# The front of an attention and ELU-MLP kernel: two token tiles side by side, one batch ahead

## The chip, the cores and the metric

The kernel runs on one core of a Trainium2 chip. The metric is the device time of one execution in microseconds. The engines in the text are PE (matrix multiply), PEld (its weight loads), DVE (vector), ACT (activations), POOL (GpSimd, which also issues DMAs that cast) and SP (issues plain DMAs). Each engine works through its own queue in order and waits on semaphores.

## The reference

```python
# q, k, v: [8 batches, 8 heads, 576 tokens, 64], float32; w_in [512, 2048]; w_out [2048, 512]
scores = (q @ k^T) / 8                       # per batch and head
scores = where(|i - j| <= 32, scores, -1e9)  # sliding window, both sides
attn   = softmax(scores)
x      = (attn @ v), heads side by side      # [4608 tokens, 512]
h      = x @ w_in
g      = where(h > 0, h, exp(min(h, 0)) - 1) # ELU
out    = g @ w_out                           # [4608, 512] float32
```

## The kernel before

**Attention.** Queries go in blocks of 64 (`QB`), nine to a batch, and two blocks make a *pair*: 36 pairs of 128 tokens. A block of 64 queries sees 128 keys, so the window is one 128 x 64 product per head. For a pair, `scores` fills `psS` (16 small matmuls), ACT exponentiates into `pu`, DVE multiplies with a mask (`mask`, into `pm`), `pv` multiplies with V, which carries a column of ones for the sum, `normalize` divides (`rc`, `x_st`), `x_transpose` turns the result on PE and `x_evac` copies it into `xT`. Two pairs make the 256 tokens of one tile. The softmax takes no maximum away, and masked places are multiplied by zero.

V is held twice: `V_e` for even blocks, as loaded, and `V_o` for odd ones, shifted by 64 tokens. `rotate_v` makes `V_o` from `V_e` with two DMAs on SP's queue.

q and k are loaded as float32 by SP (`load_qk`, whole or in halves `HALF_A` and `HALF_B` of 288 tokens), cast to bf16 (`cast_qk`), transposed on PE in 96 x 96 pieces (`transpose_qk`, into a PSUM tile `ptx`) and copied into `qT` and `kT` on ACT or DVE. v and the weights are loaded and cast by DMAs that POOL issues (`load_v`, `load_w_in`, `load_w_out`; the weights in four chunks each). `gate` is a DMA of one element that SP issues when a certain weight chunk is in; what SP issues after it waits behind it.

**The MLP.** 18 tiles of 256 tokens, each in 8 steps; a step takes 256 of the 2048 middle columns. `mm1` makes 8 matmuls into `ps` (`psH`), ACT's exponential gives `e_sb`, DVE subtracts one (`m_sb`) and combines (`elu`, `g_sb`); `mm2` adds 4 matmuls of g and w_out to the tile's sum `psY`. After step 7 the sum is copied to `y_sb` by ACT and DVE and stored by SP.

**The order.** There is no scheduler: the order of the calls is the order on the engines. A table `tasks`, filled by `at(kk, slot, ...)`, hangs attention work into the steps of the MLP loop. In step kk the loop runs:

```python
    LAG = 2
    for kk in range(NSTEP + LAG):
        run(kk, "first")
        if 1 <= kk <= NSTEP:
            elu(kk - 1)
        run(kk, "dve")
        if kk < NSTEP:
            mm1(kk)
        run(kk, "mid")
        if kk >= LAG:
            mm2(kk - LAG)
        run(kk, "end")
```

`pair_at(i, kk)` spreads a pair over the steps kk to kk + 3. From pair 6 on, pair i starts at step 4(i - 2), so a pair runs every four steps.

Before the loop stand half A of batch 0, its transposes, and pairs 0 and 1, each finished before the next begins. Half B of batch 0 is cast and transposed at step 2, just ahead of that step's `elu` and `mm1`. Batch 1 is cast mostly on POOL, in steps 8 to 13.

Of the kernel before, what the change touches and what calls it, by code (L numbers as in the profile page):

```python
# [21 lines left out]
def kernel(  # L22
# [43 lines left out]
    xpool = ctx.enter_context(tc.tile_pool(name="xT", bufs=2))  # L66
    mpool = ctx.enter_context(tc.tile_pool(name="moe", bufs=3))
    opool = ctx.enter_context(tc.tile_pool(name="outs", bufs=2))
    psH_pool = ctx.enter_context(
        tc.tile_pool(name="psH", bufs=3, space=bass.MemoryType.PSUM))  # L70
    psY_pool = ctx.enter_context(
        tc.tile_pool(name="psY", bufs=1, space=bass.MemoryType.PSUM))
    psS_pool = ctx.enter_context(
        tc.tile_pool(name="psS", bufs=1, space=bass.MemoryType.PSUM))
    psT_pool = ctx.enter_context(
        tc.tile_pool(name="psT", bufs=1, space=bass.MemoryType.PSUM))
# [65 lines left out]
    for i in range(3):  # L142
        nc.vector.memset(V_e[i][0:32, 0], 0.0)
        nc.vector.memset(V_e[i][96:128, VS - 1], 0.0)
        nc.vector.memset(V_e[i][:, :, :, D:VD], 1.0)
        if i < 2:
            nc.vector.memset(kT[i][:, :, 0:WIN], 0.0)
            nc.vector.memset(kT[i][:, :, KW - WIN:KW], 0.0)

    load_qk(0, 0, HALF_A)  # L150
    load_qk(0, 1, HALF_A)
    for m in range(3):
        load_v(0, m)
    rotate_v(0, 0, 2)

    ident = cpool.tile([128, 128], BF16)
    make_identity(nc, ident)

# [21 lines left out]
    for ki, kk in enumerate(kinds):  # L180
        for z in range(2):
            nc.vector.tensor_copy(
                masks[:, ki, z, :], mk[:, "EFL".index(kk[z]), :])
# [8 lines left out]
    def cast_qk(b, which, hp, part, eng):  # L192
        z, nj = part
        n = H * nj * D
        s_ = qk_f[b, which][:, z * n + 2 * hp * nj * D:
                            z * n + (2 * hp + 2) * nj * D]
        s_ = _bap(s_, [s_.ap[0], [nj * D, 2], [D, nj], [1, D]])
        t = lpool.tile([SP_, SJ, 2, D], BF16, tag=f"b{which}", name="qkb",
                       bufs=4)
        qk_b[b, which, hp, z] = t  # L200
        d_ = _bap(t, [t.ap[0], [D, 2], [2 * D, nj], [1, D]])
        if eng is nc.scalar:
            nc.scalar.copy(d_, s_)
        else:
            eng.tensor_copy(d_, s_)  # L205

    def transpose_qk(b, which, hp, part, evac, pool=None):
        z, nj = part
        src = qk_b.pop((b, which, hp, z))
        if pool is None:  # L210
            pt = psT_pool.tile([128, SJ, SP_], BF16, tag="pt", name="ptx")
        else:
            pt = psH_pool.tile([128, 2 * 512], BF16, tag="psH", name="ptx")
            pt = _bap(pt, [pt.ap[0], [SP_, SJ], [1, SP_]])
        for j in range(nj):
            nc.tensor.transpose(  # L216
                pt[:, j, :], src[:, j, :, :], ident[0:SP_, 0:SP_])
        src_ps = _bap(pt, [pt.ap[0], [1, SP_], [SP_, nj]])
        n = SP_ * nj
        if which == 0:  # L220
            d = qT[b % 2][:, hp, z * n:(z + 1) * n]
        else:
            d = kT[b % 2][:, hp, WIN + z * n:WIN + (z + 1) * n]
        d = _bap(d, [d.ap[0], [nj, SP_], [1, nj]])
        if evac is nc.scalar:
            nc.scalar.copy(d, src_ps)  # L226
        else:
            nc.vector.tensor_copy(d, src_ps)
# [3 lines left out]
    def scores(i):  # L232
        psS = psS_pool.tile([128, 2, 512], FP32, tag="psS")
# [13 lines left out]
        st[i] = [psS, pu, None, None]  # L247

    def mask(i):
        psS, pu, _, _ = st[i]  # L250
# [6 lines left out]
    def pv(i):  # L257
        psS, pu, pm, _ = st[i]
# [23 lines left out]
    def x_transpose(i):  # L282
        psS, _, _, x_st = st[i]
        pt = psS_pool.tile([128, NDO, 128], BF16, tag="psS", name="psXT")
# [21 lines left out]
    for hp in range(HP):  # L306
        cast_qk(0, 0, hp, HALF_A, nc.vector)
        cast_qk(0, 1, hp, HALF_A, nc.scalar)
        transpose_qk(0, 0, hp, HALF_A, nc.scalar, psH_pool)
        transpose_qk(0, 1, hp, HALF_A, nc.vector, psH_pool)  # L310

    load_w_in(0)
    load_w_out(0)
    gate(w_in_at(0))
    for which in range(2):
        load_qk(0, which, HALF_B)
    for m in range(3, VS):
        load_v(0, m)
    rotate_v(0, 2, VS - 1)
    for c in range(1, 4):  # L320
        load_w_in(c)
        load_w_out(c)
    gate(w_in_at(3))
    for part in (HALF_A, HALF_B):
        for which in range(2):
            load_qk(1, which, part)
    for m in range(VS):
        load_v(1, m)
    rotate_v(1)
# [25 lines left out]
    for i in (0, 1):  # L355
        for fn in (scores, mask, pv, normalize, x_transpose, x_evac):
            fn(i)


    for hp in range(HP):  # L360
        at(2, "first", cast_qk, 0, 0, hp, HALF_B, nc.vector)
        at(2, "first", cast_qk, 0, 1, hp, HALF_B, nc.scalar)
        at(2, "first", transpose_qk, 0, 0, hp, HALF_B, nc.scalar)
        at(2, "first", transpose_qk, 0, 1, hp, HALF_B, nc.vector)
    at(2, "first", scores, 2)
    at(3, "dve", mask, 2)
    at(3, "mid", pv, 2)
    at(4, "dve", normalize, 2)
    at(4, "mid", x_transpose, 2)
    at(5, "dve", x_evac, 2)  # L370
    pair_at(3, 5)

    for hp in range(HP):
        at(8 + hp // 2, "mid", cast_qk, 1, 0, hp, HALF_A, nc.scalar)
        at(8 + hp // 2, "mid", cast_qk, 1, 1, hp, HALF_A, nc.gpsimd)
        at(9 + hp // 2, "mid", transpose_qk, 1, 0, hp, HALF_A, nc.scalar)
        at(9 + hp // 2, "mid", transpose_qk, 1, 1, hp, HALF_A, nc.scalar)
        at(12 + hp // 2, "mid", cast_qk, 1, 0, hp, HALF_B, nc.gpsimd)
        at(12 + hp // 2, "mid", cast_qk, 1, 1, hp, HALF_B, nc.gpsimd)
        at(14 + hp // 2, "mid", transpose_qk, 1, 0, hp, HALF_B, nc.scalar)  # L380
        at(14 + hp // 2, "mid", transpose_qk, 1, 1, hp, HALF_B, nc.scalar)
    pair_at(4, 10)
    pair_at(5, 13)
    for i in range(6, NPAIR):
        pair_at(i, HALF * (i - 2))
    for b in range(2, B):
        k0 = HALF * (first_pair(b) - 2)
        for hp in range(HP):
            for which in range(2):
                kk = k0 + HALF * (hp - 4) + 1 + 2 * which  # L390
                at(kk - 5, "mid", cast_qk, b, which, hp, WHOLE, nc.gpsimd)
                at(kk, "mid", transpose_qk, b, which, hp, WHOLE, nc.scalar)
        at(k0 - HALF, "mid", rotate_v, b)
        if b >= 3:
            kk = k0 - 8 * HALF
# [6 lines left out]
    psH, e_t, m_t, g_t, psY = {}, {}, {}, {}, {}  # L402

    def mm1(kk):
        t, s = kk // STEPS, kk % STEPS
        ps = psH_pool.tile([128, FG, TT], FP32, tag="psH")
# [23 lines left out]
    def mm2(kk):  # L430
        t, s = kk // STEPS, kk % STEPS
        if s == 0:
            psY[t] = [psY_pool.tile([128, D_MODEL], FP32, tag=f"psY{ts}",
                                    name=f"psY{ts}")
                      for ts in range(2)]
# [57 lines left out]
```

## Time and profile before

| | |
|---|---|
| device time, median of 3 | 379.85 us (378.91 to 381.76) |
| the profiled execution, its own time | 378.95 us |
| its span, first to last instruction | 377.2 us |
| PE busy | 328.4 us (87%) |
| DVE busy | 254.1 us (67%) |
| ACT busy | 169.4 us (45%) |
| POOL busy | 88.5 us (23%) |
| mean granted PE clock | 0.959 |
| DMA, over the span | 42.01 MB, 111 GB/s |

A row of the timeline gives start and length in microseconds, engine, source line, operation, what is written and read, the number of instructions, and in brackets how long the engine was idle before it and what ended that. `x16` merges neighbours of one kind. A row of the stages gives start and end, then length and busy time of each engine. A row of groups gives busy time and mean nanoseconds of one, then the idle time before them. SPq and POOLq are the queues of DMAs that those engines issue.

### The profile page before, as it was taken

To read this page: it belongs to the slowest core of one execution; us is meant where nothing else is said; L and a number is where in the kernel's file an instruction comes from. 1 tells how busy PE (TensorE), PEld (TensorE's weight loads), DVE (VectorE), ACT (ScalarE), POOL (GpSimd) and SP (SyncE) were. 2 spreads that over 40 slices of the span, in tenths; PEclk is the share of its full clock that TensorE was granted. 3 is DMA by queue.
4 is the path that set the end of the run, shared out by engine and by line. 5 is a ranking of instruction groups with operands and counts; after the bars stand their busy time and mean duration, and the time that the engine had idled before them with its cause. 6 is when DMAs were issued, how large, how long until landed. Compare 5 with 4: busy or idle time off the path is not lost.

```text
span 377.2 us, 8269 instructions
## 1 busy us (share of the span) xinstructions
PE 328.4 (87%) x3408; PEld 216.6 (57%) x3408; DVE 254.1 (67%) x488; ACT 169.4 (45%) x284; POOL 88.5 (23%) x123
## 2 busy tenths in 40 slices
PE   0443885586999999999999999999999999999994
PEld 0232553354566666666666666666666666666662
DVE  5334574062588777778888787788787777777773
ACT  1414236243445555545545454445554554444431
POOL 6632310428216131042242061412110000000000
PEclk9997799596899999999999999999999999999999
DMA  9999999709929956592093939394010301101011
GB/s 161 170 230 223 173 230 209 164 1 223 123 81 109 219 157 40 112 211 69 2 154 27 250 71 151 64 236 132 2 60 2 112 2 57 45 13 58 2 56 56
DMA packets 63785, 42.01 MB, mean 111 GB/s; under 512 B 38532, under 2 KB 57988, under 8 KB 63748
## 3 DMA queue, kind: packets, MB, share of 16 engines
q1 hardware_dynamic: 22020, 32.57, 35.2%
q0 software_dynamic: 41728, 8.92, 29.9%
q8 instruction: 26, 0.43, 0.5%
q14 instruction: 11, 0.09, 0.1%
HBM read 36.70 MB, written 9.44 MB: 122 GB/s over the span
## 4 chain that ended last, share of the span: by engine, by line
PE 71%; DMA 10%; DVE 8%; ACT 4%; issue 3%; POOL 1%; SPq 0%; DVEq 0%; POOLq 0%; ACTq 0%
PE ps L411 30%; PE psY L439 28%; PE ptx L216 5%; DMA f<-in_q_dram 5%; DMA f<-in_k_dram 4%; PE psS L239 3%; PE psXT L286 3%; PE psS L265 2%; ACT e_sb L417 2%; DVE g_sb L424 2%; DVE y_sb L448 2%; DVE x_st L277 2%; DMA w_in_sb<-in_moe_w_in_dram 1%; ACT qT L226 1%; DVE m_sb L419 1%
## 5 line engine op out<-in xcount | busy, mean ns | idle before, releaser
L417 ACT ACTIVATE e_sb<-ps 128x512 f32<-128x512 f32 x144 | 86.0, 597 | 166.6 <-PE ps L411 166.5
L411 PE MATMUL ps<-xT,w_in_sb 128*128 128x256 bf16 x1152 | 153.7, 278 | 2.1 <-DVE xT L296 2.1
L439 PE MATMUL psY<-w_out_sb,g_sb 128*128 128x512 bf16 x576 | 150.6, 385 | 0.2 <-DVE g_sb L424 0.2
L411 PEld LDWEIGHTS <-w_in_sb 128*128 128x128 bf16 x1152 | 110.6, 100 | 33.8 <-issue 3.1
L419 DVE TENSOR_SCALAR m_sb<-e_sb 128x512 bf16<-128x512 f32 x144 | 71.8, 499 | 64.2 <-ACT e_sb L417 63.8
L424 DVE SCALAR_TENSOR_TENSOR g_sb<-ps,m_sb 128x512 bf16<-128x512 f32 x144 | 99.4, 690 | 13.5 <-DVE m_sb L419 0.5
L205 POOL CAST qkb<-f 96x768 bf16<-96x768 f32 (+1 forms) x60 | 46.6, 799 | 133.7 <-PE ptx L216 70.8
L439 PEld LDWEIGHTS <-g_sb 128*128 128x128 bf16 x576 | 51.3, 99 | 39.5 <-issue 2.1
L216 PE MATMUL ptx<-ident,qkb 96*128 96x96 bf16 x384 | 31.8, 218 | 31.4 <-DVE qkb L205 16.0
L108 POOL DMA_DIRECT2D Ve<-in_v_dram x40 | 33.6, 846 | 54.1 <-PE psS L265 35.1
L216 PEld LDWEIGHTS <-qkb 96*128 96x128 bf16 x384 | 25.0, 103 | 36.4 <-DVE qkb L205 17.5
L245 ACT ACTIVATE pu<-psS 128x1024 bf16<-128x1024 f32 x36 | 36.7, 1019 | 7.8 <-PE psS L239 7.6
L253 DVE TENSOR_TENSOR pm<-pu,masks 128x1024 bf16<-128x1024 bf16 x36 | 25.1, 698 | 11.7 <-ACT pu L245 11.7
L277 DVE TENSOR_TENSOR x_st<-psS,rc 128x512 bf16<-128x512 f32 x36 | 24.9, 692 | 1.2
L226 ACT COPY qT<-ptx 128x576 bf16<-128x576 bf16 (+1 forms) x40 | 21.5, 538 | 8.0 <-PE ptx L216 7.8
L265 PEld LDWEIGHTS <-pm 128*64 128x64 bf16 x576 | 12.8, 114 | 19.4 <-issue 10.2
L226 ACT COPY kT<-ptx 128x576 bf16<-128x576 bf16 (+1 forms) x32 | 18.4, 575 | 9.4 <-PE ptx L216 9.4
L265 PE MATMUL psS<-Ve,pm 128*64 128x65 bf16 x320 | 16.9, 201 | 4.2 <-DVE pm L253 4.2
L286 PEld LDWEIGHTS <-x_st 128*128 128x128 bf16 x144 | 9.7, 101 | 16.8 <-DVE x_st L277 13.9
L296 DVE COPY xT<-psXT 128x512 bf16<-128x512 bf16 x36 | 15.0, 416 | 5.8 <-PE psXT L286 5.8
L286 PE MATMUL psXT<-ident,x_st 128*128 128x128 bf16 x144 | 14.8, 228 | 3.9 <-DVE x_st L277 3.5
L239 PE MATMUL psS<-qT,kT 64*128 64x64 bf16 x576 | 16.0, 196 | 1.6 <-DVE xT L296 1.0
(30 smaller groups left out, 84.3 us busy)
## 6 DMA issues: line engine op xcount, KB each, us to landing
out_dram<-y_sb SPq DMA_DIRECT2D x18, 512.0 KB, 3.1
f<-in_q_dram SPq DMA_DIRECT2D x6, 1152.0 KB, 10.6
f<-in_k_dram SPq DMA_DIRECT2D x6, 1152.0 KB, 15.0
Vo<-Ve SPq DMA_DIRECT2D x14, 260.0 KB, 4.6
Ve<-in_v_dram POOLq DMA_DIRECT2D x24, 128.0 KB, 7.8
f<-in_q_dram SPq DMA_DIRECT2D x4, 576.0 KB, 9.9
f<-in_k_dram SPq DMA_DIRECT2D x4, 576.0 KB, 16.8
w_in_sb<-in_moe_w_in_dram POOLq DMA_DIRECT2D x4, 512.0 KB, 16.8
```

What stands on the lines that cost most here:

```text
L108: nc.gpsimd.dma_start(out=V_e[b % 3][p0:p1, m, :, 0:D], in_=v[b, :, lo + p0:lo + p1, :].rearrange("h p d -> p h d"))
L205: eng.tensor_copy(d_, s_)
L216: nc.tensor.transpose(pt[:, j, :], src[:, j, :, :], ident[0:SP_, 0:SP_])
L226: nc.scalar.copy(d, src_ps)
L245: nc.scalar.activation(pu, _bap(psS, [psS.ap[0], [1, 1024]]), AX.Exp, scale=SCALE)
L265: nc.tensor.matmul(psS[QB * z:QB * (z + 1), par, hp * VD:(hp + 1) * VD], lhsT=pm[:, par * HP + hp, z * QB:(z + 1) * QB], rhs=vv[:, qb // 2 ...
L286: nc.tensor.transpose(pt[:, do, :], x_st[:, 2 * do:2 * do + 2, :], ident)
L411: nc.tensor.matmul(ps[:, j, :], lhsT=w_in_sb[:, do, fo * 128:(fo + 1) * 128], rhs=xT[t][:, do, :], start=(do == 0), stop=(do == NDO - 1))
L417: nc.scalar.activation(e_sb, ps, AX.Exp)
L419: nc.vector.tensor_scalar(m_sb, e_sb, -1.0, None, ALU.add)
L424: nc.vector.scalar_tensor_tensor(g_sb, psH.pop(kk), 0.0, m_t.pop(kk), ALU.max, ALU.min)
L439: nc.tensor.matmul(psY[t][ts], lhsT=g_sb[:, j, ts * 128:(ts + 1) * 128], rhs=w_out_sb[:, s * FG + j, :], start=(s == 0 and j == 0), stop=( ...
```

## The change

It has five parts.

1. *Loads.* SP issues all of q and k of batch 0, both halves, at once, POOL all five pieces of its v. Then come weight chunks 0 and 1, a gate on chunk 1, half A of batch 1, chunks 2 and 3, a gate, half B of batch 1, and batch 2.
2. *The front.* q and k of batch 0 are cast and transposed for two head pairs at a time (one PSUM tile of two half banks). Pairs 0 and 1 go through the attention side by side, in two PSUM buffers. Then half B, the scores and masks of pairs 2 and 3, and only then step 0; the rest of pairs 2 and 3 is done in steps 0 to 2.
3. *The order of steps.* Tiles 0 and 1 take turns: tile 0's steps 0 and 1, tile 1's steps 0 and 1, then step n of both for n from 2 to 7. From step 16 on all is as before.
4. *PSUM.* One pool with named buffers: h0, h1, h2 (one bank each), t0 (one), s and y (two each). `ps` uses h0 and h1 until step 17, and then all three; tile 1's sum lives in h2 and t0, that of all other tiles in y, as one tile of two banks. `xT` has three buffers.
5. *Batch 1 and 2.* Batch 1 is cast for all heads at once, q on ACT and k on DVE, in steps 6 and 15, and transposed through buffer s, 12 transposes and one wide copy on ACT each. Pairs 4 to 7 start at steps 9, 12, 18 and 21 (before 10, 13, 16, 20). Batch 2 is cast by POOL from step 18 and transposed in steps 20 to 27 (before from step 13). Pads and masks of DVE move behind half A's transposes.

```diff
-    for i in range(3):
+    def pads(i):
...
+    for part in (HALF_A, HALF_B):
+        for which in range(2):
+            load_qk(0, which, part)
+    for m in range(VS):
+        load_v(0, m)
...
+    def front_qk(part):
+        for g in range(2):
+            hps = (2 * g, 2 * g + 1)
+            cast_qk(0, 0, part, hps, nc.vector)
+            cast_qk(0, 1, part, hps, nc.scalar)
+            transpose_qk(0, 0, part, hps, nc.scalar, ("h0", "h1")[g])
+            transpose_qk(0, 1, part, hps, nc.vector, ("h2", "t0")[g])
...
-    for i in (0, 1):
-        for fn in (scores, mask, pv, normalize, x_transpose, x_evac):
+    for i, tag in ((0, "s"), (1, "y")):
+        scores(i, tag)
+    for fn in (mask, pv, normalize, x_transpose, x_evac):
+        for i in (0, 1):
             fn(i)
...
+    front_qk(HALF_B)
+    for i, tag in ((2, "s"), (3, "y")):
+        scores(i, tag)
+        mask(i)
+    for i in (2, 3):
+        at(0, "mid", pv, i)
+        at(1, "dve", normalize, i)
+        at(1, "mid", x_transpose, i)
+        at(2, "dve", x_evac, i)
...
+    order = [(0, 0), (0, 1), (1, 0), (1, 1)]
+    order += [(z, n) for n in range(2, STEPS) for z in range(2)]
+    order += [(t, n) for t in range(2, NT) for n in range(STEPS)]
...
+        t, s = order[kk]
+        h = kk % 2 if kk < 18 else (kk + 2) % 3
+        ps = psum.tile([128, FG, TT], FP32, tag=f"h{h}", name="ps")
```

**SP's queue at the start.** `f_116` and `f_118` (before), `f_104` and `f_106` (after) hold q and k of batch 0; `f_224` and `f_226`, `f_194` and `f_196` those of batch 1; `Vo_97` and `Vo_88` are batch 0's shifted V. Before:

```order
L99 DMA f_116<-in_q_dram 96x8x192
L99 DMA f_118<-in_k_dram 96x8x192
L114 DMA Vo_97<-Ve_94 64x1040
L115 DMA Vo_97<-Ve_94 64x1040
L123 DMA gate_t<-w_in_sb 1x1
L99 DMA f_116<-in_q_dram 96x8x192
L99 DMA f_118<-in_k_dram 96x8x192
L114 DMA Vo_97<-Ve_94 64x1040
L115 DMA Vo_97<-Ve_94 64x1040
L123 DMA gate_t<-w_in_sb 1x1
L99 DMA f_224<-in_q_dram 96x8x192
```

And of the change:

```order
L94 DMA f_104<-in_q_dram 96x8x192
L94 DMA f_106<-in_k_dram 96x8x192
L94 DMA f_104<-in_q_dram 96x8x192
L94 DMA f_106<-in_k_dram 96x8x192
L109 DMA Vo_88<-Ve_85 64x1040
L110 DMA Vo_88<-Ve_85 64x1040
L109 DMA Vo_88<-Ve_85 64x1040
L110 DMA Vo_88<-Ve_85 64x1040
L118 DMA gate_t<-w_in_sb 1x1
L94 DMA f_194<-in_q_dram 96x8x192
L94 DMA f_196<-in_k_dram 96x8x192
```

The second half of q and k has moved ahead of the first rotation and its gate is gone; half A of batch 1 has moved ahead of the second gate.

**DVE's queue from half B to the third step.** `qkb` are the casts of q, `kT` the copies of k, `pm` the masks' products, `m_sb` and `g_sb` the ELU. Before:

```order
L419 TENSOR_SCALAR m_sb<-e_sb 128x512
L424 SCALAR_TENSOR_TENSOR g_sb<-ps,m_sb 128x512
L419 TENSOR_SCALAR m_sb<-e_sb 128x512
L205 CAST qkb<-f_116 96x2x3x64
L228 COPY kT_92<-ptx 128x288
L205 CAST qkb<-f_116 96x2x3x64
L228 COPY kT_92<-ptx 128x288
```

And of the change:

```order
L193 CAST qkb<-f_104 96x4x3x64
L193 COPY kT_83<-ptx 128x2x288
L252 TENSOR_TENSOR pm<-pu,masks 128x1024 x2
L431 TENSOR_SCALAR m_sb<-e_sb 128x512
L436 SCALAR_TENSOR_TENSOR g_sb<-ps,m_sb 128x512
L273 RECIPROCAL rc<-psS 128x8
L276 TENSOR_TENSOR x_st<-psS,rc 128x512
L273 RECIPROCAL rc<-psS 128x8
L276 TENSOR_TENSOR x_st<-psS,rc 128x512
L431 TENSOR_SCALAR m_sb<-e_sb 128x512
L436 SCALAR_TENSOR_TENSOR g_sb<-ps,m_sb 128x512
L295 COPY xT<-psXT 128x4x128 x2
```

Half B's casts and copies stood between the m_sb of step 1 and its g_sb; now they stand ahead of the first m_sb, and the two normalisations of pairs 2 and 3 stand between the steps 0 and 1.

198 lines of the change are left out of this document (90 added, 108 removed).

## The prediction

> **What bounds the kernel now.** I first read the page for the span, then busy time by stage, because the kernel is not one thing: the first hundred microseconds and the rest have different limits.
>
> ```profile
> span 377.2 us, 8269 instructions
> 0.00:26.00 26.00, 6.88 (x96) 4.75 (x97) 11.27 (x38) 6.75 (x12) 15.38 (x31) 1.00 1.32 183
> 26.00:40.00 14.00, 6.79 (x54) 4.26 (x54) 5.11 (x13) 4.42 (x10) 3.31 (x4) 0.72 1.28 219
> 40.00:63.00 23.00, 19.35 (x181) 12.47 (x178) 12.82 (x25) 10.13 (x19) 3.67 (x5) 0.95 1.57 202
> 63.00:72.00 9.00, 1.99 (x29) 1.37 (x27) 1.85 (x4) 2.28 (x6) 1.73 (x3) 0.69 1.12 237
> 72.00:101.00 29.00, 24.16 (x212) 14.79 (x206) 11.99 (x22) 11.80 (x23) 16.22 (x23) 0.74 0.92 106
> 101.00:118.00 17.00, 16.83 (x191) 11.51 (x191) 13.96 (x25) 8.61 (x15) 5.89 (x8) 1.00 0.39 75
> ```
>
> After the length of a stretch stand the busy times of PE, its weight loads, DVE, ACT and POOL, then the granted PE clock and the DMA share. From 101 us on PE is full: 16.83 of 17.00. Before that it idles 41.8 of 101 us, and where it works the clock is down (0.72, 0.69, 0.74). So only the front can gain, and the rest runs at PE's own pace. The output copies of ACT mark that pace tile by tile:
>
> ```profile
> 100.97 0.60 ACT L447 COPY y_sb<-psY 128x512 f32<-128x512 f32 x1
> 118.58 0.61 ACT L447 COPY y_sb<-psY 128x512 f32<-128x512 f32 x1
> ```
>
> Tile 1 is done at 101.0, tile 2 at 118.6, 17.6 later. By step 25, where tile 2 ends, both kernels have put out nearly the same attention work. So the plan of the sum is: find when tile 2 ends in the changed kernel, and leave the 258.7 us behind it (377.2 - 118.6) as they are. The timeline shows what PE idles for:
>
> ```profile
> 0.81 0.39 SPq L99 DMA_DIRECT2D f<-in_q_dram  x1
> 8.92 0.35 DVE L205 CAST qkb<-f 96x384 bf16<-96x384 f32 x1
> 10.20 0.54 SPq L114 DMA_DIRECT2D Vo<-Ve  x1
> 10.96 0.46 SPq L115 DMA_DIRECT2D Vo<-Ve  x1
> 14.58 0.46 DVE L228 COPY kT<-ptx 128x288 bf16<-128x288 bf16 x1 [0.76 <-PE ptx L216]
> 18.12 0.26 PE L265 MATMUL psS<-Vo,pm 128*64 128x65 bf16 x1 [0.47 <-DMA Vo<-Ve]
> 20.45 0.42 DVE L296 COPY xT<-psXT 128x512 bf16<-128x512 bf16 x1 [0.70 <-PE psXT L286]
> 26.19 3.19 PE L411 MATMUL ps<-xT,w_in_sb 128*128 128x256 bf16 x16 [0.52 <-DVE xT L296]
> 30.73 0.34 DVE L205 CAST qkb<-f 96x384 bf16<-96x384 f32 x1
> 39.33 0.46 DVE L228 COPY kT<-ptx 128x288 bf16<-128x288 bf16 x1 [1.40 <-PE ptx L216]
> 68.12 1.73 POOL L205 CAST qkb<-f 96x768 bf16<-96x768 f32 x3 [14.99 <-DMA f<-in_q_dram]
> 69.45 0.42 PE L216 MATMUL ptx<-ident,qkb 96*128 96x96 bf16 x3 [6.04 <-POOL qkb L205]
> ```
>
> Two pairs go through the attention one after the other until 26.2; two steps later PE waits until 39.8 for the second half of batch 0; at 63 it waits 6.04 us for batch 1, whose casts stand on POOL behind a cast of batch 2 that waited 14.99 us for its load. The weights were not what came last here.
>
> **The change, step by step.** *Half A.* q lands 4.9 us after its issue, 5.7:
>
> ```profile
> DMA to landing us min/median/max: 4.9/10.6/16.8
> 7.97 1.02 DVE L182 CAST masks<-mk 128x64 bf16<-128x64 f32 x8 [2.38 <-POOL mk L171]
> 0.97 0.49 DVE L143 MEMSET Ve<- 32x520 bf16 x1 [0.97 <-PEq L477]
> 2.57 0.49 DVE L143 MEMSET Ve<- 32x520 bf16 x1
> ```
>
> The mask casts, which held DVE until 8.99, now stand behind the transposes, so the first cast starts at 5.8, not 8.9. Before, half A took 6.1 us (8.92 to 15.04) in four rounds; two rounds of double width wait for k's landing too (ACT's first cast at 9.14 is its upper bound, I take 7.3), so I count 7.6: ready at 13.4. Then DVE owes the mask casts, 1.0, and two sets of pads at 1.6 each (0.97 to 2.57), before it may mask: 17.7, and the first mask is done at 18.4. The exponentials are done by then. That is 4.2 us of DVE work moved onto the path, unless something else is later.
>
> *V_o.* It is. The two DMAs that rotate V go out when their third of V has landed, and came in 6.9 and 7.1 us later (the max in the row is the second half's):
>
> ```profile
> DMA to landing us min/median/max: 6.9/9.6/13.1
> f<-in_q_dram SPq DMA_DIRECT2D x4, 576.0 KB, 9.9
> ```
>
> V landed at 10.2 and 10.96, with nothing but itself on the queues after q and k were in. Now the second halves of q and k, 2 x 576 KB, are issued right behind the first on SP and share the DMA engines with V. Floor: no delay, 10.96. Ceiling: V waits the whole 6 us or so that the first halves needed before. I take 4.1, since V starts while the first halves still run: 15.1, and 7.0 for the rotation: 22.2. With the shortest rotation of these tiles in the front, 3.7, it would be under the 18.4 of the masks. So the products with V start at 22.3, between 18.5 and 25.
>
> *To the first weight matmul.* One pair took 2.75 us from its first product with V_o to its finished xT (18.12 to 20.87). Two side by side add one normalisation and one copy (0.20 + 0.69 + 0.42, with hand-offs 1.55): 4.3. Then half B: all of it is now ahead of the first matmul. It took 9.1 us before (30.73 to 39.79), tangled with other work; 6.1 for half A; I take 6.5. Two score blocks at the low clock, 1.4. Sum: 22.3 + 4.3 + 6.5 + 1.4 = 34.5. The first weight matmul is 8.3 us *later* than today's 26.19.
>
> *Steps 0 to 2.* Pairs 2 and 3 are still to be finished, and step 2 needs their xT. This is DVE's queue:
>
> ```profile
> L253 DVE TENSOR_TENSOR pm<-pu,masks 128x1024 bf16<-128x1024 bf16 x7 | 5.1, 730 | 11.7 <-ACT pu L245 11.7
> L277 DVE TENSOR_TENSOR x_st<-psS,rc 128x512 bf16<-128x512 f32 x6 | 4.2, 692 | 0.2
> L274 DVE RECIPROCAL rc<-psS 128x8 f32<-128x8 f32 x6 | 1.2, 203 | 4.6 <-PE psS L265 4.6
> L296 DVE COPY xT<-psXT 128x512 bf16<-128x512 bf16 x6 | 2.5, 420 | 5.8 <-PE psXT L286 5.8
> L419 DVE TENSOR_SCALAR m_sb<-e_sb 128x512 bf16<-128x512 f32 x18 | 8.8, 487 | 17.7 <-ACT e_sb L417 17.6
> L424 DVE SCALAR_TENSOR_TENSOR g_sb<-ps,m_sb 128x512 bf16<-128x512 f32 x17 | 11.7, 690 | 1.6
> ```
>
> Two each: 2 x (0.73 + 0.69 + 0.20 + 0.42 + 0.49 + 0.69) = 6.4 us, plus 1.8 of hand-offs and the first exponential: 8.2. Step 2 starts at 42.7; PE does only two blocks of mm1 and small work in this time.
>
> *Steps 2 to 17, side by side.* From the full-clock stretch:
>
> ```profile
> 105.84 0.87 PE ps L411 x8
> 106.71 0.34 PE psS L239 x16
> 109.15 0.86 PE psY L439 x4
> 110.01 0.38 PE psS L265 x16
> 112.24 0.24 PE psXT L286 x4
> 113.35 0.26 PE ptx L216 x6
> ```
>
> Until tile 1 ends there are 16 mm1 blocks (13.9), 16 mm2 blocks (13.8), eight groups of six transposes of batch 1 (2.1) and pairs 4 and 5 at 0.34 + 0.38 + 0.24 (1.9): 31.7. Two buffers for ps instead of three: a buffer comes back after ACT's 0.60, DVE's 0.49 and 0.69 and some 0.3 of hand-offs, 2.1 us, while PE has 0.86 + 0.87 + 0.86 = 2.6 us of other work. That holds by 0.5, except where a wide cast of batch 1 (96 x 1536, four times the 0.35 on DVE and 0.51 on ACT, fewer fixed costs) or a wide evacuation goes between; for those and the copies of pairs 4 and 5 I add 2.5. Tile 1's copy: 42.7 + 34.2 = 76.9, or 77.1 behind ACT's evacuation.
>
> Are the loads in time? SP's second gate waits for the last chunk of w_in, so its issue dates the landing:
>
> ```profile
> 38.33 0.61 SPq L123 DMA_DIRECT2D gate_t<-w_in_sb  x1
> ```
>
> Chunk 3 of w_in was in by 38.3. Now the rest of batch 0 is ahead of all chunks and the first part of batch 1 ahead of chunks 2 and 3, another 1.18 MB of q and k, and V: at the 200 GB/s of the stage rows 6 us for q and k, 12 with V. Chunk 3 then comes by 51. Step 12, its first user, starts at 42.7 + 10 x 1.73 + 2 or more, 62. So the weights are covered, and would have been with less interleaving.
>
> *Clock.* PE rests for some 3 us between its second and third mm1. The rows above give three dips of about 10 us at half (1 - 0.72, 0.69, 0.74 of their stretches, doubled: 7.8, 5.6 and 15.1, with 2.3 from the row between, 30.8 in all); they follow pauses of 6 us or thin work. A dip here would cost from 0 to 5.1 us, as PE is the bound. I take 1.7, a third, since the pause is short. [...] Tile 1: 78.8.
>
> *Step 18.* It reuses the bank of tile 1's sum, so mm1 waits for ACT's copy behind a wide evacuation, 1.4. Pair 6's scores and products (0.34 + 0.38) and two groups of batch 2 (0.5) have moved behind this point. So tile 2 takes 17.6 + 1.4 + 0.7 + 0.5 = 20.2 and ends at 99.0, against 118.6.
>
> *Costed at nothing.* POOL issues all of V ahead of the selects that make the masks (two more issues): the masks' casts come at 13.4 now, behind q and k, which is the cover; without it DVE would start them some 2 us later than before. SP sends q and k of batch 1 only behind four rotations and a gate: nobody needs them before step 6. The sum of a tile is one buffer of two banks now, so the next tile's first mm2 waits for both copies; DVE's is an evacuation like g_sb's 0.69, and an mm1 block of 0.87 lies between, which leaves nothing over only at the last tile, where no attention work remains (0.1). A third xT buffer and ps's three buffers from step 18 on take no time. The casts that leave POOL end the wait at 63, whose worth is in the sum already, as nothing of before's stages is carried over.
>
> Sum: 19.6 us earlier. The profiled execution took 378.95 (span 377.2 and 1.75 around it), so 359.3; the median of three runs is 0.9 above it, and I predict 360.
>
> **The rivals.** *V arrives early.* If q and k's second halves do not delay V and the rotation takes 3.7, the masks decide at 18.5, and with no clock dip and little stall the gain is 19.6 + 3.7 + 1.7 = 25: 354. For it: the first loads came in fast. Against: the DMA share is 1.1 or more in each stage up to 72.
>
> *The front stretches.* Half B takes its old 9.1 (+2.6), V_o comes at 25 (+2.7), a dip lasts 10 us (+3.4): all of it gives 8.7 back, 368. For it: the same work took that long today.
>
> *The loads of batch 1 hit PE.* This one ends on the other side. Its casts are on ACT and DVE now, with the step's own e_sb and g_sb queued behind them, where POOL could wait alone before. Half A is cast in step 6, at about 50. It is issued when w_in's chunk 1 is in, about 25; PE stops for each microsecond that it lands after 50, and beyond 50 + 19.6 = 70 (or half B beyond step 15's 68 + 19.6 = 88) the kernel is slower than today. Batch 2's q took 17.2 us, landing at 68 from an issue at 50.75; such a load from 25 lands at 42, so it would have to queue behind all the weights and then some. If half A waits for chunk 3's old gate and half B for 20 us more, 38.3 + 17.2 = 56 costs 6 us, 366. To reach 390 both must slip by 20 us.
>
> *The rotation of roles buys nothing.* If the front is bound by bytes, all of batch 0 instead of half of it, the gain is what the removed wait at 63 gives alone, 6 us and part of the dip after it: 370.
>
> **How the numbers follow.** The step sum, 355 to 364, 0.58; early V, 0.14; the stretched front and the byte-bound one, 364 to 373, 0.20; within 1% (3.8 us, about what a measurement of this kernel can tell from no change), 0.04; slower, from batch 1's loads, 0.04. The range takes in the first three up to the bounds of V_o, half B and clock: 350 to 369.
>
> **What would show it.** The first weight matmul near 34 and not before 26; PE waiting for V_o at about 18 to 22; tile 1 copied near 79 and tile 2 near 99, with tile 0 only one step ahead of tile 1; no wait on POOL's casts near 63; a granted clock of 1.00 from about 50 on; from tile 2 on some 17 us per tile, as now. A cast of batch 1 with idle time before it that a DMA ended would prove the rival of the loads, and a first matmul at 30 or less the early V. The forecast fails if PE's rest stretches beyond step 2 or if the pace per tile changes.

## The result, and the profile after

The changed kernel takes 361.72 us (median of 4 runs, 361.45 to 362.94) against 380.81 us before (4 runs, 378.91 to 382.17): a ratio of 0.951, 95% interval 0.946 to 0.956. The forecast was 360, in a range of 350 to 369. The total is right, but by luck, for two parts of the sum are not: the front came out 5.6 us better than forecast, and 8.0 us were lost again behind it, in a step that I had costed at nothing.

The page and the busy time by stage, in the same stretches as before (columns: from:to and its length, the busy times of PE, its weight loads, DVE, ACT and POOL with the numbers of their instructions, granted PE clock, DMA share, GB/s):

```profile
span 360.1 us, 8168 instructions
26.00:40.00 14.00, 9.31 (x121) 6.67 (x121) 7.96 (x16) 5.73 (x8) 4.93 (x6) 1.00 1.42 211
40.00:63.00 23.00, 22.01 (x223) 15.01 (x224) 15.69 (x30) 11.91 (x16) 1.65 (x2) 1.00 1.52 210
63.00:72.00 9.00, 8.36 (x74) 5.78 (x77) 7.44 (x14) 6.22 (x9) 6.09 (x7) 1.00 0.88 150
72.00:101.00 29.00, 25.68 (x303) 17.60 (x308) 21.02 (x37) 15.60 (x26) 15.64 (x19) 1.00 1.05 202
101.00:118.00 17.00, 16.43 (x185) 11.02 (x186) 14.01 (x24) 8.22 (x15) 5.77 (x8) 1.00 1.38 185
```

The front is what changed: PE works 22.01 of 23 us between 40 and 63 where it worked 19.35, 8.36 of 9 between 63 and 72 where it worked 1.99, and the granted clock stands at 1.00 in each stretch. The last row is the warning: between 101 and 118, where PE was full before (16.83 of 17.00), it now works 16.43.

The timeline of the front shows each step of the sum (columns: start, duration, engine, line, operation, output and input; in brackets the idle time before it and what ended it):

```profile
12.56 0.76 DVE L193 COPY kT<-ptx 128x576 bf16<-128x576 bf16 x1 [1.23 <-PE ptx L215]
17.05 0.73 DVE L252 TENSOR_TENSOR pm<-pu,masks 128x1024 bf16<-128x1024 bf16 x1
21.39 0.26 PE L264 MATMUL psS<-Vo,pm 128*64 128x65 bf16 x1 [3.29 <-DMA Vo<-Ve]
24.89 0.55 DVE L193 CAST qkb<-f 96x768 bf16<-96x768 f32 x1
29.12 0.76 DVE L193 COPY kT<-ptx 128x576 bf16<-128x576 bf16 x1 [1.23 <-PE ptx L215]
30.80 1.89 PE L423 MATMUL ps<-xT,w_in_sb 128*128 128x256 bf16 x8
38.11 1.03 PE L423 MATMUL ps<-xT,w_in_sb 128*128 128x256 bf16 x8 [1.39 <-DVE xT L295]
71.96 0.59 ACT L462 COPY y_sb<-psY 128x512 f32<-128x512 f32 x1
93.39 0.59 ACT L462 COPY y_sb<-psY 128x512 f32<-128x512 f32 x1
```

Half A is ready at 13.3, the first mask is done at 17.8, and PE then waits 3.29 us for the rotated V. Half B takes 24.89 to 29.88. The first weight matmul is at 30.80, step 2 at 38.11, tile 1 ends at 71.96 and tile 2 at 93.39, 25.2 us before the 118.58 of the kernel before.

The same stretch as one row, from the start to ACT's copy of tile 2, before and then after:

```profile
0.00:118.58 118.58, 76.58 (x746) 49.25 (x747) 57.40 (x124) 44.57 (x83) 46.20 (x73) 0.87 1.12 160
0.00:93.39 93.39, 64.90 (x737) 45.09 (x748) 57.22 (x118) 42.00 (x60) 35.56 (x54) 1.00 1.34 201
```

With nearly the same number of matmuls, PE is idle for 28.5 us where it was idle for 42.0, and busy for 64.9 where it was busy for 76.6. So 13.5 of the 25.2 us are waits that are gone, and 11.7 are the same work done in less time, at a clock of 1.00 in place of 0.87.

Of those 25.2 us the span keeps 17.1 (377.2 - 360.1). The end of a tile shows where the other 8 went. First the kernel before, behind ACT's copy at 118.58, then the changed kernel at its next tile:

```profile
118.69 0.69 DVE L448 COPY y_sb<-psY 128x512 f32<-128x512 f32 x1
119.30 0.68 DVE L424 SCALAR_TENSOR_TENSOR g_sb<-ps,m_sb 128x512 bf16<-128x512 f32 x1
119.85 1.03 PE L439 MATMUL psY<-w_out_sb,g_sb 128*128 128x512 bf16 x4
```

```profile
111.48 0.59 ACT L462 COPY y_sb<-psY 128x512 f32<-128x512 f32 x1
112.09 0.69 DVE L463 COPY y_sb<-psY 128x512 f32<-128x512 f32 x1 [0.20 <-ACT y_sb L462]
112.70 0.68 DVE L436 SCALAR_TENSOR_TENSOR g_sb<-ps,m_sb 128x512 bf16<-128x512 f32 x1
112.84 1.02 PE L454 MATMUL psY<-w_out_sb,g_sb 128*128 128x512 bf16 x3
```

Before, DVE's copy starts 0.11 us after ACT's, beside it. Now it starts 0.61 us after it, when ACT is done. Everything behind it on DVE moves by as much, the next g_sb first, and PE's next product into the sum starts when DVE's copy has ended. The groups of the page say that this is so at nearly each tile (the last columns: idle time before the group, and what ended most of it):

```profile
L463 DVE COPY y_sb<-psY 128x512 f32<-128x512 f32 x18 | 12.4, 690 | 9.5 <-ACT y_sb L462 9.5
```

From ACT's copy of tile 2 to its copy of tile 17 it takes 261.4 us now and took 253.3 before. The order of the program has the reason in writing, for it lists what each instruction waits for. The same copy of DVE, in the kernel before and in the changed one:

```
L448 COPY y_sb<-psY_1145 128x512 [waits DMAHW2_49,PE_49]
L463 COPY y_sb<-psY 128x512 [waits DMAHW4_49,Activation_49]
```

With a tile for each half, DVE waits for PE. With one tile of two banks it waits for ACT, its fellow reader. In the kernel before, the two copies run side by side for 0.50 us (118.69 to 119.19), each in its own tile. The runs show what the wait costs; whether the chip needs it, and what reads without it would do in one tile, they do not show.

### The profile page after: what moved, and what is told of

Read it like the earlier page. It is cut to its first block, busy times and chain, and to the rows that moved or that the text cites. A ratio compares the mean times of both kernels' runs of the same rounds, so it can differ in the third digit from the quotient of the medians.

```text
span 360.1 us, 8168 instructions
## 1 busy us (share of the span) xinstructions
PE 316.8 (88%) x3356; PEld 212.4 (59%) x3408; DVE 255.7 (71%) x482; ACT 168.7 (47%) x262; POOL 84.1 (23%) x111
## 4 chain that ended last, share of the span: by engine, by line
PE 67%; DVE 16%; ACT 8%; DMA 5%; issue 3%; POOL 0%; DVEq 0%
PE ps L423 30%; PE psY L454 26%; DVE g_sb L436 4%; PE ptx L215 4%; DVE x_st L276 4%; DVE y_sb L463 3%; DMA Ve<-in_v_dram 3%; PE psS L238 3%; ACT y_sb L462 3%; PE psXT L285 3%; ACT e_sb L429 2%; PE psS L264 2%; ACT qT L191 2%; DVE m_sb L431 2%; DMA Vo<-Ve 2%
## 5 line engine op out<-in xcount | busy, mean ns | idle before, releaser
L423 PE MATMUL ps<-xT,w_in_sb 128*128 128x256 bf16 x1152 | 150.5, 274 | 3.6 <-DVE xT L295 2.7
L454 PE MATMUL psY<-w_out_sb,g_sb 128*128 128x512 bf16 x524 | 141.1, 379 | 4.3 <-DVE y_sb L463 0.5
L423 PEld LDWEIGHTS <-w_in_sb 128*128 128x128 bf16 x1152 | 108.9, 98 | 33.8 <-issue 4.0
L193 POOL CAST qkb<-f 96x768 bf16<-96x768 f32 x48 | 42.1, 899 | 117.1 <-PE ptx L215 55.0
L215 PE MATMUL ptx<-ident,qkb 96*128 96x96 bf16 x384 | 27.7, 215 | 13.0 <-DVE qkb L193 10.3
L215 PEld LDWEIGHTS <-qkb 96*128 96x128 bf16 x384 | 23.5, 102 | 15.6 <-DVE qkb L193 11.0
L252 DVE TENSOR_TENSOR pm<-pu,masks 128x1024 bf16<-128x1024 bf16 x36 | 26.6, 742 | 2.0 <-ACT pu L244 1.9
L191 ACT COPY qT<-ptx 128x576 bf16<-128x576 bf16 (+1 forms) x30 | 20.0, 666 | 12.7 <-PE ptx L215 12.7
L463 DVE COPY y_sb<-psY 128x512 f32<-128x512 f32 x18 | 12.4, 690 | 9.5 <-ACT y_sb L462 9.5
L264 PE MATMUL psS<-Vo,pm 128*64 128x65 bf16 x256 | 14.6, 202 | 4.0 <-DMA Vo<-Ve 3.3
L191 ACT COPY kT<-ptx 128x576 bf16<-128x576 bf16 (+1 forms) x26 | 17.4, 670 | 0.0
## 6 DMA issues: line engine op xcount, KB each, us to landing
f<-in_q_dram SPq DMA_DIRECT2D x6, 1152.0 KB, 11.7
w_in_sb<-in_moe_w_in_dram POOLq DMA_DIRECT2D x4, 512.0 KB, 17.1
```

What stands on the lines that cost most here:

```text
L215: nc.tensor.transpose(pt[:, g, j * SP_:(j + 1) * SP_], src[:, j, g * 128:(g + 1) * 128], ident[0:SP_, 0:SP_])
L264: nc.tensor.matmul(psS[QB * z:QB * (z + 1), par, hp * VD:(hp + 1) * VD], lhsT=pm[:, par * HP + hp, z * QB:(z + 1) * QB], rhs=vv[:, qb // 2 ...
L423: nc.tensor.matmul(ps[:, j, :], lhsT=w_in_sb[:, do, fo * 128:(fo + 1) * 128], rhs=xT[t][:, do, :], start=(do == 0), stop=(do == NDO - 1))
L454: nc.tensor.matmul(psY[t][ts], lhsT=g_sb[:, j, ts * 128:(ts + 1) * 128], rhs=w_out_sb[:, s * FG + j, :], start=(s == 0 and j == 0), stop=( ...
```

## The experiments

Theory: the front gained what the sum of steps says and a little more, and the sum in one tile takes some 0.5 us of each tile back. Rivals: the tiles slowed for another reason (the moved work of batch 2, two `ps` buffers, the turns of tiles 0 and 1), or the front's gain was the removed wait at 63 us alone.

**The joint sum alone, in the kernel before.**

```diff
-            psY[t] = [psY_pool.tile([128, D_MODEL], FP32, tag=f"psY{ts}",
-                                    name=f"psY{ts}")
-                      for ts in range(2)]
+            y = psY_pool.tile([128, 2, D_MODEL], FP32, tag="y", name="psY")
+            psY[t] = [y[:, 0, :], y[:, 1, :]]
```

> The kernel before, with a tile's sum psY held in one tile of two banks instead of two tiles, as in the change; nothing else. Theory (the pace per tile fell because the two evacuations of one tile follow each other: DVE's copy starts only when ACT's is done, and g_sb and the next tile's first mm2 stand behind it): DVE's copy starts some 0.6 us later, the pace goes from 16.9 to about 17.4 us a tile, 16 or 17 tiles of it make 8 us, 389. Rival (the pace fell for another reason in the change, such as the order of pairs or the named banks): the time stays at 380.8 within 1%.

Measured: 387.15 us against 379.64, ratio 1.018 (1.011 to 1.025). In its timeline DVE's copy waits for ACT's as in the changed kernel:

```profile
120.01 0.58 ACT L446 COPY y_sb<-psY 128x512 f32<-128x512 f32 x1
120.62 0.69 DVE L447 COPY y_sb<-psY 128x512 f32<-128x512 f32 x1 [0.68 <-ACT y_sb L446]
```

Tile 2 to tile 17 takes 261.4 us here, the changed kernel's figure to 0.1. So this one edit, with nothing else, gives the whole loss of pace: 7.5 us.

**The sum in two tiles, in the changed kernel.** The buffer y becomes y0 and y1; pairs 1 and 3, whose scores use the same banks in the front, do their exponential and normalisation in two halves.

```diff
-                y = psum.tile([128, 2, D_MODEL], FP32, tag="y", name="psY")
-                psY[t] = [y[:, 0, :], y[:, 1, :]]
+            psY[t] = [psum.tile([128, D_MODEL], FP32, tag=g, name="psY")
+                      for g in (("h2", "t0") if t == 1 else ("y0", "y1"))]
```

> The changed kernel, with each sum psY in two tiles of one bank again, as before; pairs 1 and 3, which use the same two banks, take two exponentials, two reciprocals and two multiplications instead of one each. Theory (joint sum): the pace is 16.9 a tile again, 8 us less, and the doubled instructions of two pairs cost under 1 us: 354. Rival (another reason): the pace stays at 17.4, time 361 to 363.

Measured: 355.37 us, ratio 0.934 (0.928 to 0.940), 6.3 us below the changed kernel. The copies stand side by side again:

```profile
130.64 0.61 ACT L485 COPY y_sb<-psY 128x512 f32<-128x512 f32 x1
130.75 0.69 DVE L486 COPY y_sb<-psY 128x512 f32<-128x512 f32 x1
```

From tile 2 to tile 17 it takes 255.1 us, and 253.5 in a second execution, which the last section compares with this one; the kernel before took 253.3. So the pace is back, and from both sides the joint sum is worth 6 to 7.5 us. Its theory stands, with somewhat less than the 8 us that it named. This kernel beats both.

**No turns of tiles 0 and 1.**

```diff
-    order = [(0, 0), (0, 1), (1, 0), (1, 1)]
-    order += [(z, n) for n in range(2, STEPS) for z in range(2)]
-    order += [(t, n) for t in range(2, NT) for n in range(STEPS)]
+    order = [(t, n) for t in range(NT) for n in range(STEPS)]
```

> The changed kernel with tile 0's eight steps first and then tile 1's; loads, front and buffers as in the change. Theory (the weights were covered by half a batch of work ahead of them, so taking turns buys nothing): chunk 2 is used at step 4, near 42 us, and had landed at 36 and 40; chunk 3 at step 6, near 45 and 48.5, and had landed at 43.9 and 47.9: 361 to 363. Rival (the turns are what keeps PE from waiting for weights): PE stops at steps 4 and 6 for some 4 us or more: 366.

Measured: 362.09 us, ratio 0.951 (0.945 to 0.957), the changed kernel's own. The ACT copies of its tiles 0 and 2:

```profile
53.40 0.59 ACT L460 COPY y_sb<-psY 128x512 f32<-128x512 f32 x1
92.56 0.58 ACT L460 COPY y_sb<-psY 128x512 f32<-128x512 f32 x1
```

Tile 0 ends 16 us sooner, tile 1 (at 72.16) and tile 2 about when they did. The side-by-side order that gives the change its name buys nothing that can be measured: the weights are there in time without it, and no wait of PE for a weight load shows in this trace.

**Two `ps` buffers to the end.**

```diff
-        h = kk % 2 if kk < 18 else (kk + 2) % 3
+        h = kk % 2
```

> The changed kernel with two buffers for ps in all steps, not only in the first 18. Theory (a buffer comes back after 2.1 us, PE has 2.6 us of other work): 361 to 363 in the whole. Rival (two buffers stall PE whenever attention work stands on ACT or DVE): 0.1 to 0.2 us a step over 126 steps, 375 to 387, and then the side-by-side steps paid the same, 2 to 3 us.

Measured: 362.21 us, ratio 0.952 (0.944 to 0.959), no difference from the changed kernel's 0.951. The third buffer takes no time away, as costed.

**Batch 2 late, in the kernel before.**

```diff
+                ahead = 5
+                if b == 2:
+                    kk, ahead = 20 + HP * which + hp, 2
-                at(kk - 5, "mid", cast_qk, b, which, hp, WHOLE, nc.gpsimd)
+                at(kk - ahead, "mid", cast_qk, b, which, hp, WHOLE, nc.gpsimd)
```

> The kernel before with one thing altered: GpSimd's casts and the transposes of batch 2 go to steps 18 to 27, as the change has them, in place of the steps where they stood; the attention of batches 0 and 1 stays where it was. Theory: the wait of 6 us at 63 us in the profile before (a GpSimd cast of batch 1 stands behind one of batch 2, which waits for its load) goes, and part of the half-clock stretch behind it with it: 6 to 8.5 us less, about 372 us. Rival: the next wait (the attention of batch 1 between the tiles) takes its place and at most 2 us go, 378 us or more. By the theory the rest of the change in the front, the attention of batch 0 and the weights under it, is worth some 17 us when the sum y in one piece is put back in two.

Measured: 373.16 us against 377.86, ratio 0.988 (0.983 to 0.992), 4.6 us. That lies between the two: more than the rival's 2, less than the 6 to 8.5. The POOL casts that stood 14.99 us behind a load of batch 2 now wait for PE only, and tile 2 ends here:

```profile
63.91 0.50 POOL L205 CAST qkb<-f 96x384 bf16<-96x384 f32 x1 [1.35 <-PE ptx L216]
111.48 0.60 ACT L450 COPY y_sb<-psY 128x512 f32<-128x512 f32 x1
```

In this execution tile 2 is 7.1 us earlier; over the runs it is less. So of the change's 19.1 us the moved casts give some 4.6, the joint sum takes 6.3 to 7.5, and if the parts add up, 21 to 22 us are left for the rest of the front. That rest is several things at once: all of batch 0 loaded and transposed ahead of the first weight step, its attention in pairs side by side, and batch 1's casts on ACT and DVE in place of POOL. No run here takes them apart; the two rows up to tile 2 split the 25.2 us into waits and clock, but not by part of the change.

**What bounds the front now.** V first: the odd halves of V of batch 0 come straight from memory, in place of the rotations, on the kernel with the sum in two tiles. That makes four more loads on POOL's queue. The later pieces of V are now issued behind the selects of the masks and the last one behind the first weight chunks, and a memset writes the ones column of `V_o`; the lines below show only the new load and the rotations that it replaces.

```diff
+    def load_v_odd(b, m):
+        lo = 128 * m + WIN
+        nc.gpsimd.dma_start(
+            out=V_o[b % 3][:, m, :, 0:D],
+            in_=v[b, :, lo:lo + 128, :].rearrange("h p d -> p h d"))
...
-    rotate_v(0, 0, 2)
-    rotate_v(0, 2, VS - 1)
```

> The changed kernel with the sum y in two tiles of a bank, and with the odd halves of V of batch 0 loaded from memory by GpSimd itself in place of the rotations from the even halves. Theory: the products with V wait 3.3 us for the rotated half in the profile after (21.4 against 18.1), and that wait sets the front; without it they begin with the mask at about 18, and all that follows moves 3 to 3.6 us ahead: about 352 us against 355.4 with the sum in two tiles alone. Rival: the added V loads delay the second halves of q and k or the weights by as much, or half B of the keys is what the first products wait for: 354.5 to 357 us.

Measured: 352.86 us, but its ratio, 0.933 (0.930 to 0.937), does not differ from the 0.934 of its base, which ran on another chip. So both were run again on one chip.

> The changed kernel with the sum y in two tiles of a bank once more, the base on one chip for the two runs beside it. All theories: about 0.934 of the kernel before.

> The odd halves of V of batch 0 loaded from memory, beside its base on the same chip: on two chips the ratios could not be told apart (0.9333 and 0.9339), while the profiled spans differ by 2.5 us. Theory (the rotated half of V sets the front): 2 to 3 us below the base. Rival (V is not what comes last, the profiled difference is one of two executions): within 0.7 us of it.

Measured: the base 355.16 us, ratio 0.939 (0.936 to 0.941); V loaded directly 353.40, ratio 0.934 (0.931 to 0.937). That is 1.8 us, under the theory's 2 to 3 and above the rival's 0.7; the intervals of the two ratios overlap by a little. The wait for V is gone, and the first weight matmul moves from 30.59 to 28.14. The base, with its load of batch 1's k, its first step and its step 4:

```profile
27.95 0.55 SPq L94 DMA_DIRECT2D f<-in_k_dram  x1
30.59 1.89 PE L450 MATMUL ps<-xT,w_in_sb 128*128 128x256 bf16 x8
41.67 1.04 PE L450 MATMUL ps<-xT,w_in_sb 128*128 128x256 bf16 x8
```

And V loaded directly, with the same rows, step 3 and step 8:

```profile
18.38 0.26 PE L285 MATMUL psS<-Ve,pm 128*64 128x65 bf16 x1 [3.62 <-DVE pm L273]
28.14 1.89 PE L458 MATMUL ps<-xT,w_in_sb 128*128 128x256 bf16 x8
30.19 0.56 SPq L94 DMA_DIRECT2D f<-in_k_dram  x1
38.63 1.87 PE L458 MATMUL ps<-xT,w_in_sb 128*128 128x256 bf16 x8
41.20 1.04 PE L458 MATMUL ps<-xT,w_in_sb 128*128 128x256 bf16 x8
47.77 1.05 DVE L201 CAST qkb<-f 96x1536 bf16<-96x1536 f32 x1 [0.97 <-DMA f<-in_k_dram]
49.47 1.03 PE L458 MATMUL ps<-xT,w_in_sb 128*128 128x256 bf16 x8 [0.16 <-DVE g_sb L471]
```

What became of the 2.45 us? In these two executions 2.15 are left at step 2 (36.05 for 38.20), 0.47 at step 4 and 0.14 at step 8, and the spans are 351.7 and 351.4. Most of it goes between steps 2 and 4, where PE has half the clock for a while in this execution (step 3 takes 1.87 us, not 1.04, and the clock is 0.89 from 26 to 40 us) and full clock in the base's (1.00). The base has executions with such a dip too: in the first run of the sum in two tiles, step 7 starts at 48.63, here at 46.41, and 2.2 us of the lead are still there. So the 1.8 us rest on the medians, not on this pair of profiles. A new wait shows as well: DVE's cast of batch 1's k, in step 6, waits 0.97 us for its load, which costs PE 0.16 us. The edit itself has delayed this load, much as its rival warned: it is issued 2.2 us later than in the base, behind a gate on weight chunk 1, and POOL now issues three more loads of V ahead of that chunk.

**VectorE's pads behind the masks.**

```diff
     for i in (0, 1):
         mask(i)
+    pads(1)
+    pads(2)
```

> The kernel of the run with V loaded directly, and VectorE's pads of batches 1 and 2 (some 2 us) moved behind the masks of pairs 0 and 1. Theory: with V off the path the masks are what the first products with V wait for; the first mask ends near 15.6 in place of 17.8, and 1 to 2 us more go: about 350 us. Rival: V itself, landing at 14 to 16 or later in this order, or the second half of the keys is the bound: no change against the run with V loaded directly, within 0.7 us.

Measured: 354.01 us, ratio 0.936 (0.932 to 0.940), no gain over the 352.86 us of V loaded directly on this chip. The products start 2 us sooner and lose it to the same pads, which now hold up the normalisation, and the first weight matmul comes at 29.02, against 27.97:

```profile
16.21 0.26 PE L285 MATMUL psS<-Ve,pm 128*64 128x65 bf16 x1 [1.42 <-DVE pm L273]
21.02 0.61 PE L320 MATMUL psXT<-ident,x_st 128*128 128x128 bf16 x4 [3.18 <-DVE x_st L310]
```

**The pads in steps 3 to 11.**

```diff
+    at(3, "mid", pads, 1, 0)
+    at(4, "mid", pads, 1, 1)
+    at(5, "mid", loads_2)
+    at(8, "mid", pads, 2, 0)
+    at(11, "mid", pads, 2, 1)
```

> V loaded directly, and VectorE's pads of batches 1 and 2 moved out of the front into steps 3 to 11, with the second part of batch 1's loads behind step 5. Moved behind the masks alone they gave nothing: the first products with V began 2 us sooner (16.2), but the normalisation then waited 3.2 us for the same pads. Theory: VectorE's queue sets the front once V is there, so 2 to 3 us go now, first weight matmul near 25.5 and about 350 us. Rival: the second half of q and k, or the first weights, is next behind it: within 0.7 us of the run with V loaded directly.

The lines above leave out that each set of pads is split in two. `loads_2` holds the second part of batch 1's loads and those of batch 2.

Measured: 369.48 us, ratio 0.977 (0.974 to 0.979): 16 us worse than without the edit, a miss of my making. The first weight matmul did come at 25.25, as the theory says. Then:

```profile
72.43 0.73 DVE L477 SCALAR_TENSOR_TENSOR g_sb<-ps,m_sb 128x512 bf16<-128x512 f32 x1 [12.52 <-DMA Ve<-in_v_dram]
72.56 0.09 DVE L148 MEMSET Ve<- 128x40 bf16 x1
73.55 0.61 PE L254 MATMUL psS<-qT,kT 64*128 64x64 bf16 x16 [13.43 <-DVE xT L332]
```

The memset of batch 2's ones column stood behind the loads of the same tile in the code, so it waited for them, 12.5 us, with DVE's whole queue behind it and PE behind that. The idle time is printed at g_sb, whose row starts 0.13 us ahead of the memset's; but in DVE's queue the memset stands ahead of g_sb, and no load has anything to do with g_sb. Behind the wait PE's first weight block, at 75.77, takes 1.55 us and the next, at 78.50, 1.05. The mean granted clock is 0.968 in this execution and 0.994 without the edit.

**The memset ahead of the loads.**

```diff
-    at(5, "mid", loads_2)
-    at(8, "mid", pads, 2, 0)
-    at(11, "mid", pads, 2, 1)
+    at(5, "mid", pads, 2, 0)
+    at(6, "mid", pads, 2, 1)
+    at(6, "mid", loads_2)
```

> As the run with the pads of batches 1 and 2 in steps 3 to 11, with the pads of batch 2 in steps 5 and 6, ahead of its V loads in the code. In that run the first weight matmul came at 25.3, 2.9 us sooner than without the edit, but the memset of batch 2's ones column stood behind the loads of the same tile and held VectorE for 12.5 us. Theory: with the memset ahead of the loads the 13 us go, and step 2 keeps its 3 us: about 350.5 us, 0.926 of the kernel before. Rival: the weights or VectorE's steps 3 to 6 take the 3 us back, 353 us as with V loaded directly.

Measured: 354.67 us, ratio 0.934 (0.930 to 0.938). The 13 us are back, the 3 us are not: the rival holds, with another place than I named.

```profile
26.02 1.89 PE L464 MATMUL ps<-xT,w_in_sb 128*128 128x256 bf16 x8
47.49 1.23 DVE L203 CAST qkb<-f 96x1536 bf16<-96x1536 f32 x1 [2.38 <-DMA f<-in_k_dram]
49.37 1.36 PE L464 MATMUL ps<-xT,w_in_sb 128*128 128x256 bf16 x8 [2.72 <-DVE g_sb L477]
```

In three kernels the first weight matmul is at 30.59, 28.14 and 26.02, and the cast of batch 1's k starts at 47.19 (no wait), 47.77 (0.97) and 47.49 (2.38). In the first of them the load had landed by about 45.4, 17.4 us after its issue; in the other two it is issued some 2 us later (30.19 and 29.77) and decides when the cast starts. From the second kernel to the third, step 7 comes 2.7 us sooner (43.75 for 46.41) and step 8 only 0.1 (49.37 for 49.47): g_sb stands behind the cast on DVE, and PE waits 2.72 us for it. What the front gains is waited away there. No run issues this load sooner, so what lies behind it is not shown.

**Narrow rounds again.** q and k of batch 0 in four rounds of two heads per half, as before the change, on the kernel with V loaded directly.

```diff
-        for g in range(2):
-            hps = (2 * g, 2 * g + 1)
+        for g in range(4):
+            hps = (g,)
```

> The kernel with V loaded directly, and q and k of batch 0 cast and transposed in four rounds of two heads per half again, in place of two rounds of four. Theory: the wide rounds save fixed costs and hand-offs: a half takes about 6.1 us in four rounds by the kernel before and 4.8 to 5.0 in two by the changed one, so the first weight matmul comes 2 to 2.6 us later, and the time is 2 to 2.5 us longer, about 355.5. Rival: the rounds overlap on four buffers, what counts is elements, and the difference is within 0.7 us.

Measured: 354.76 us, ratio 0.936 (0.933 to 0.939).

```profile
30.36 1.89 PE L458 MATMUL ps<-xT,w_in_sb 128*128 128x256 bf16 x8
```

The first weight matmul is 2.2 us later, as the theory has it, but the time is 0.6 us longer by the ratios, whose intervals overlap: it can be told neither from none nor well from 2 us. In the two profiled executions the 2.2 us are gone by step 8 (49.35 here, 49.47 with wide rounds). Of them 1.7 go between steps 2 and 4, where the wide kernel's execution has the half clock and this one has not (0.89 and 1.00 from 26 to 40 us), and 0.3 behind them, where the cast waits for the load of batch 1 (0.31 us here, 0.97 there). Whether wide rounds save time over many executions stays open.

## Why the prediction was right, and where it was wrong

*Half A and the masks.* Forecast 13.4 and 18.4, measured 13.3 and 17.8. Right.

*V_o.* Right as the bound and nearly in time: PE waits for it until 21.39, forecast 22.3. The rotation's row in the changed kernel gives the delay itself:

```profile
DMA to landing us min/median/max: 5.3/5.5/5.7
```

V came in at 14.9, forecast 15.1; I took 7.0 for the rotation and it was 5.5.

*To the first weight matmul.* 9.4 us from the products with V_o, forecast 12.2. Two pairs took 3.6 for 4.3, half B 5.0 for 6.5, the two score blocks 0.9 for 1.4. Half B was mis-sized by the old kernel's four narrow rounds; the run with narrow rounds confirms that they bring the first weight matmul 2.2 us later, over both halves. Steps 0 to 2 took 7.3 for 8.2, steps 2 to 17 33.9 for 34.4.

*Clock.* Forecast 1.7 for a dip behind step 1, measured 0 in the changed kernel's profile; of PE's some 3 us between the second and the third mm1, only the last 1.39 are all idle. The term is not nothing in general: in one execution of the last section it is 1.7 us. The three dips of the kernel before, 30.8 us at half clock, are gone, and the sum had this in it without a line of its own, as it took the steps' prices from the stretch at full clock.

*Step 18 and tile 2.* 21.4 for 20.2; with the sum in two tiles it is 20.2 and 20.8, so part of this is the joint sum already. The sum of these differences is -0.9 - 2.8 - 0.9 - 0.5 - 1.7 + 1.2, which is the 5.6 us by which tile 2 came early (93.4 for 99.0).

*Behind tile 2.* This is the step that failed. I left the 258.7 us as they are, and wrote of the sum of a tile in one buffer of two banks: "DVE's is an evacuation like g_sb's 0.69, and an mm1 block of 0.87 lies between, which leaves nothing over only at the last tile". That takes the two copies side by side. They are in series, 0.59 and then 0.69, 1.3 us against the 0.87 that covers them, and the delay of g_sb behind them comes on top: 0.3 to 0.9 us for a tile, 8.0 over the stretch (266.7). The copy's wait on ACT stood in the changed program's order before any run, and I had looked at the length of the wait, not at whom it waits for. I named the pace per tile as what would make the forecast fail; it did change, and the total held because two errors of opposite sign met. That is luck: the mechanism behind tile 2 was wrong.

*Costed at nothing, and nothing:* the third `ps` buffer and the turns of tiles 0 and 1, which the prediction gave as needless for the weights. *The rivals.* "V early" names 354, and with the tiles' pace as before the changed front does give 355.2 to 355.4 (the sum in two tiles). But its own term, 3.7 us from V, is not where that comes from: PE waited 3.29 us for V_o, and the time came out of the two pairs, half B and the steps. "The front stretches" did not occur: half B, V_o and the clock all came out better than the sum. "The rotation of roles buys nothing" is out: the moved casts alone give 4.6 of 19.1 us. "The loads of batch 1 hit PE" did not occur in the changed kernel, where half A's k landed at about 45.8 and its cast began at 47.10. But that load is the next limit: with the first weight matmul at 25.25 and at 26.02, and the load issued 1 us later, PE waited 2.77 and 2.72 us behind its cast.

## What to carry to other kernels

A PSUM tile was also a unit of waiting here: two engines that empty the halves of one tile were put one behind the other, DVE's copy 0.61 us behind ACT's, at 6 to 7.5 us for the kernel. So give each reader its own tile, and read in the program's order whom each copy waits for before costing it at the length of one. Follow a gain to the next transfer that does not move with it, and see whether the edit delays that transfer itself: here step 7 came 2.7 us sooner and step 8 only 0.1, and loading V directly had put the load in between 2.2 us later. Compare the clock of two profiles before laying a difference between them to an edit: here it made 1.7 us between two executions of one kernel. A memset written behind a load into the same tile waited 12.5 us for the load, and everything queued behind the memset waited too.

## What the runs showed of the hardware

Two executions of one and the same kernel, the one with the sum in two tiles, on two chips, differ by 2.8 us in span (354.2 and 351.4). One place in the front gives 1.75 us: step 7 begins at 48.63 and at 46.88. PE's third weight block, the stretch ahead of it and the stretch that it begins, in the first execution:

```profile
38.41 1.87 PE L450 MATMUL ps<-xT,w_in_sb 128*128 128x256 bf16 x8 [1.46 <-DVE xT L322]
34.80:38.20 3.40, 1.20 (x12) 0.62 (x11) 3.23 (x9) 0.60 (x1) 0.89 (x1) 1.00 1.18 232
38.20:41.60 3.40, 2.97 (x11) 1.72 (x12) 0.71 (x3) 0.60 (x1) 0.87 (x1) 0.50 1.17 233
```

and in the second:

```profile
38.20 1.03 PE L450 MATMUL ps<-xT,w_in_sb 128*128 128x256 bf16 x8 [1.43 <-DVE xT L322]
38.20:41.60 3.40, 3.35 (x23) 2.34 (x24) 1.12 (x2) 1.19 (x2) 0.88 (x1) 1.00 1.17 233
```

The first has the clock at 0.50 for 3.4 us, which is 1.7 us of full speed lost; the second, with nearly the same rest of PE ahead of the block (1.43 us for 1.46), lost none. So the clock term of the prediction is one that an execution has or has not: 1.7 was its size, and 0 its value in the changed kernel's profile. The six executions of this kernel on one chip bear it out: their spans go from 351.4 to 354.4 us and their mean clocks from 0.998 to 0.990. Not all of the 2.8 us is explained by it: 1.2 are left at tile 2 (93.98 and 92.81), and behind tile 2 the first execution takes 1.6 us longer, at a clock of 1.00 in both between 95 and 120 us. In the first execution PE was busy for 1.20 of the 3.40 us ahead of the dip; what starts a dip, no run shows. In comparisons of kernels with such a rest, 1.7 us between two single profiles can be the clock alone, as in this pair; the ratios over several runs above are what the verdicts rest on.

At the start the clock column does not tell how long a matmul takes. The first weight block takes 1.89 us in eight kernels with the new front, and in the changed kernel most matmuls of it take 421 ns, where the same matmul takes 273 ns from the second or third block on. In the changed kernel the column stands at 1.00 through all of this, so in about the first 30 us the lengths of the matmuls have to be read beside it. Whether the clock is what makes them longer there, no run shows.
